# A hedgehog-attention and SwiGLU block: order of the wk transposes, evacuation of the folds, and the way of token tile 0

## The chip, the cores and the metric

One core of a Trainium2 chip runs the whole kernel. TensorE (PE in the profile) multiplies, ScalarE (ACT), VectorE (DVE) and GpSimd (POOL) do the elementwise work, and SyncE (SP) issues most of the DMAs. The metric is the device time in microseconds (us) of one execution; the median of several runs is compared.

## The reference

All values are bf16. Tokens S = 2048, width D = 640, 32 heads of 20, MLP width F = 1536.

```python
xn = layernorm(x)                        # no gain, no bias
q, k, v = split(xn @ wqkv)               # 32 heads of 20
pq, pk = q_h @ w_phi[h], k_h @ w_phi[h]  # per head, 20 x 20
phi = concat(softmax(p), softmax(-p))    # 40 features per head, for q and for k
kv, z = phi_k.T @ v, sum_s(phi_k)        # linear attention, not causal
attn = (phi_q @ kv) / (phi_q @ z + 1e-6) @ wo
mlp  = (silu(xn @ w1) * (xn @ w3)) @ w2
out  = x + attn + mlp
```

## The kernel before

Tokens lie in 16 tiles of 128. The kernel needs xn twice: by token (x_tok, normalised in place) and transposed (xnT, five chunks of 128 features by 2048 tokens), which all products with xn read. Tiles 4 to 15 are transposed by DMA (`turn`, line 693: one `dma_start_transpose` on SP). Tiles 0 to 3 are on the way to the first products, so they are handled apart: each is centred (`centre`), transposed on TensorE against an identity (`xc_transpose`) and used for the value rows (`v_pair`, `v_first`), and normalised (`ln_apply`) and transposed once more on TensorE for xnT (`xn_transpose`, line 857: five transposes into one PSUM bank, one evacuation). The tuple TURNED names those of the tiles 0 to 3 whose xnT comes by DMA instead (lines 1165 to 1171); it is empty.

The feature map w_phi is multiplied into wq and wk on the chip: `fold` (line 882) takes wq or wk transposed (wqkT, five chunks, each loaded by a transposing DMA from memory, `load_wT`, line 721) and a block-diagonal BDc that POOL builds from w_phi (phi_s), and writes Wkp (which = 1) or Wqp (which = 0). A fold uses two PSUM banks for the two halves of 320 columns, in six matmuls, and there are five folds for each of wk and wq. Key tiles (`k_tile`) are then xnT times Wkp, exponentiated on ACT; the MLP (`mlp`) works on blocks of 512 tokens and 128 of the 1536 hidden columns. Its weights w1_s and w3_s (w_s in the profile) come in four loads each of 384 columns, so the first pair allows three MLP units.

The order of the instructions is not written by hand. The function builds a list of operations with their data dependences and a level (priority) each; `_Program.schedule` (line 172) plays them on a table of prices: at each step every engine proposes the operation that could start first, and among those that could start within a small slack the one with the highest level. Where an operation has several ways (evacuations on ACT or DVE) the plan also chooses the engine. The slack is drawn at random from the seed SEED up to 175 us of planned time. The result is a fixed list for each engine, with semaphore waits. Queues are served in that order, so an instruction on SP that waits holds all DMAs behind it on SP.

The lines that set the start of the loads (`load_w13(0, 384)` issues w1's columns, then w3's):

```python
    n = len(P.all)
    load_w13(0, 384, lv - 4)
    for d in P.all[n:]:
        d.raw.add(chunk)
    first = [P.all[-1]]
    for e in range(DC):
        o = load_wT(1, e, lv - 9 - e, first)
        if e == 1:
            load(phi_s[:], phi_t, lv - 10.5, "SP", first)
    load_x(4, 8, lv - 19, "SP", [o])
```

The operations in `first` have to be complete before the wk transposes and phi are issued; the loads after them (x tiles 4 to 15, the other columns of w1 and w3, the wq transposes) wait for the last wk transpose. Levels: lv is 9e5; a transposing DMA of TURNED tiles has 2e6.

Of the kernel before, what the change touches and what calls it, by code (L numbers as in the profile page):

```python
# [4 lines left out]
ACT = mybir.ActivationFunctionType  # L5
# [5 lines left out]
D = 640  # L11
H = 32
DH = 20
F = 1536
T = S // 128
DC = D // 128
# [12 lines left out]
def heads_of_chunk(c):  # L29
    return (128 * c) // DH, (128 * c + 127) // DH  # L30
# [462 lines left out]
        return lists  # L493
CENTRED = {0: "ACT", 1: "ACT", 2: "ACT", 3: "DVE"}
POOLED = ()
TURNED = ()
SEED = 222
TRIPLES = ((0, 3, 0, 60), (3, 3, 60, 60), (6, 3, 120, 60), (9, 3, 180, 60), (12, 3, 240, 60), (13, 3, 300, 20))


def bass_parallel_sum__linear_kernel_hedgehog__glu_gated_swiglu__prompt_kernel(
# [13 lines left out]
    P = _Program(nc)  # L515
# [12 lines left out]
    def new(name, shape, dtype, offset=None):  # L528
        size = mybir.dt.size(dtype)
        for n in shape[1:]:  # L530
            size *= n
        return P.sbuf(name, shape, dtype, region(size) if offset is None else offset)
# [17 lines left out]
    xnT = new("xnT", [128, DC, S], bf)  # L550
    w1_s = new("w1_s", [128, DC, F], bf)
    w3_s = new("w3_s", [128, DC, F], bf)
    Wqp = new("Wqp", [128, DC, D], bf)
# [13 lines left out]
    Wkp = new("Wkp", [128, DC, D], bf, RKV)  # L567
    wv = new("wv", [128, DC, D], bf, RKV + 6400)
# [15 lines left out]
    v2 = new("v2", [128, T, H * 21 + 2], bf, RV)  # L584
# [14 lines left out]
    def bank(k, cols=512, off=0, p0=0, p1=128):  # L599
        return PS[p0:p1, k * 512 + off:k * 512 + off + cols]  # L600

    def bank2(k, cols):
        return PS[:, k * 512:(k + 2) * 512].rearrange("p (b c) -> p b c", c=512)[:, :, 0:cols]

    def free(ap):
        n = 1
        for s in ap.shape[1:]:
            n *= s
        return n
# [6 lines left out]
    def mm(j, o, l, r, start, stop, shared=False, busy=None):  # L616
        u, n = P.unit, free(r)

        def emit():
            return nc.tensor.matmul(o(u.k), l, r, start=start, stop=stop, skip_group_check=shared)  # L620
        return P.mm(emit, [l, r], j, max(n / 2400 + 0.0025, 0.035) if busy is None else busy, n)

    def way(eng, name, args, kw, busy, lat):
        u = P.unit
        e = {"ACT": nc.scalar, "DVE": nc.vector, "POOL": nc.gpsimd}[eng]

        def emit():
            return getattr(e, name)(*[at(a, u) for a in args], **{k: at(v, u) for k, v in kw.items()})  # L628
        emit.__name__ = name
        return eng, (emit, busy, lat)  # L630
# [5 lines left out]
    def sb(*aps):  # L636
        return [a for a in aps if hasattr(a, "ap")]

    def add(ways, w, r, banks=None, level=0.0, after=(), part=False):
        o = P.op(dict(ways), sb(*w), sb(*r), banks, level, after)  # L640
        o.part = part
        return o

    def w_act(o, i, f, n, scale=1.0, bias=None):
        kw = dict(scale=scale)
        if bias is not None:
            kw["bias"] = bias
        extra = 0.2 if hasattr(scale, "ap") or bias is not None else 0.0
        return way("ACT", "activation", (o, i, f), kw, 0.06 + n / 1200 + extra, 0.17 + n / 1200 + extra)

    def w_copy(o, i, n, fast=1):
        return way("DVE", "tensor_copy", (o, i), {}, 0.07 + n / 960 / fast, 0.15 + n / 960 / fast)
# [40 lines left out]
    def turn(o, i, level=0.0, dram=False, after=()):  # L693
        d = P.dma("SP", lambda: nc.sync.dma_start_transpose(o, i), sb(o), sb(i), *pieces(o, 256),  # L694
                  1.31, level, after)
        d.extra = 1.0 if dram else 0.2
        return d
# [23 lines left out]
    def load_wT(which, e, level, after=()):  # L721
        return turn(wqkT[:, which * DC + e:which * DC + e + 1, :],
                    A_wqkv[:, which * D + 128 * e:which * D + 128 * e + 128], level, True, after)
# [77 lines left out]
    def xc_transpose(t, level):  # L801
        n = 2 if t == 0 else 1
        u = P.begin(n, level)
        u.name = f"cT{t}"
        for dc in range(DC):
            l = xc[:, t, 128 * dc:128 * dc + 128]
            j, b = (0, dc) if n == 1 or dc < 3 else (1, dc - 3)

            def emit(l=l, j=j, b=b):
                a = (u.k + j) * 1024 + 128 * b  # L810
                return nc.tensor.transpose(PSb[:, a:a + 128], l, ident[:])
            P.mm(emit, [l, ident[:]], j, 0.056, 128)
        for j, a, b in ((0, 0, DC),) if n == 1 else ((0, 0, 3), (1, 3, DC)):
            def src(k, j=j, n=b - a):
                return PSb[:, (k + j) * 1024:(k + j) * 1024 + 128 * n].rearrange("p (c n) -> p c n", n=128)
            o = xcT[:, t, a:b, :]
            add([w_act(o, src, ACT.Copy, 128 * (b - a)), w_copy(o, src, 128 * (b - a), 2)], [o], [], [j], 1e6)
# [64 lines left out]
    def fold(which, dc, level):  # L882
        u = P.begin(2, level)
        u.name = f"fold{which}.{dc}"
        first = [True, True]
        for e in range(DC):
            h0, h1 = heads_of_chunk(e)
            lo, hi = DH * h0, DH * (h1 + 1)
            for q in range(2):
                a, b = max(lo, 320 * q), min(hi, 320 * q + 320)  # L890
                if a < b:
                    mm(q, lambda k, q=q, a=a, b=b: bank(k + q, b - a, a - 320 * q),
                       wqkT[:, which * DC + e, 128 * dc:128 * dc + 128],
                       BDc[:, e, a - lo:b - lo], first[q], e == DC - 1 or (q == 0 and e == 2), True)
                    first[q] = False

        if which:
            o = Wkp[:, dc, :].rearrange("p (b c) -> p b c", c=320)

            def src(k):  # L900
                return bank2(k, 320)
        else:
            o = Wqp[:, dc, :].rearrange("p (c r i) -> p r c i", r=2, i=64)

            def src(k):
                return bank2(k, 320).rearrange("p r (c i) -> p r c i", i=64)
        add([w_act(o, src, ACT.Copy, D), w_copy(o, src, D)], [Wkp[:, dc, :] if which else Wqp[:, dc, :]], [],
            [0, 1], 1e6)

    def v_half(t, q, level):  # L910
        u = P.begin(1, level)
        u.name = f"V{t}.{q}"
        for i in range(DC):
            mm(0, lambda k: bank(k, 320), xnT[:, i, t * 128:(t + 1) * 128], wv[:, i, 320 * q:320 * q + 320],
               i == 0, i == DC - 1)
        o = v2[:, t, 336 * q:336 * q + 336].rearrange("p (h c) -> p h c", c=21)[:, :, 0:DH]

        def src(k):
            return bank(k, 320).rearrange("p (h c) -> p h c", c=DH)
        add([w_act(o, src, ACT.Copy, 320), w_copy(o, src, 320)], [o], [], [0], 1e6)  # L920

    def proj(t, w):
        for i in range(DC):
# [209 lines left out]
    n = len(P.all)  # L1133
    load_w13(0, 384, lv - 4)
    for d in P.all[n:]:
        d.raw.add(chunk)
    first = [P.all[-1]]
    for e in range(DC):
        o = load_wT(1, e, lv - 9 - e, first)
        if e == 1:  # L1140
# [2 lines left out]
    n = len(P.all)  # L1143
# [14 lines left out]
    n = len(P.all)  # L1158
# [6 lines left out]
    for t in range(4):  # L1165
        if t in CENTRED:
            xc_transpose(t, 6e4 - 10 * t + 15)
        if t in TURNED:
            turn(xnT[:, :, t * 128:(t + 1) * 128], x_tok[:, t, :], 2e6)
# [18 lines left out]
    for dc in range(DC):  # L1188
        fold(1, dc, 4e4 - dc)
# [5 lines left out]
    n = len(P.all)  # L1195
# [3 lines left out]
    for dc in range(DC):  # L1199
        fold(0, dc, when(60 + 2 * dc))  # L1200
# [3 lines left out]
    for b in range(3):  # L1204
        for fc in range(FC):
            n = 12 * b + fc
# [6 lines left out]
    for b in range(NB):  # L1213
        for j in range(4):
            t = 4 * b + j
# [6 lines left out]

    P.schedule({"PE": 1.25, "ACT": 1.12, "DVE": 0.93, "POOL": 0.8, "SP": 0.81}, filler, 12.0, SEED, 175.0)

# [60 lines left out]
```

## Time and profile before

| | |
|---|---|
| median of 6 runs | 275.78 us (274.56 to 278.1) |
| profiled execution | 277.8 us, its span 276.1 us |
| mean TensorE clock of it | 0.994 of full |
| PE busy | 269.2 us, 97% of the span |
| DVE, ACT, POOL busy | 181.7, 105.0, 60.7 us |
| DMA | 21.98 MB, 31% of 16 engines for the hardware queue |

The profile names an instruction by engine, source line, operation and what it writes from what it reads; most instructions come from two helper lines, L620 (matmuls) and L628 (everything on ACT, DVE and POOL), so the names of the tiles tell them apart. L690 is a plain load or store, L694 a transposing DMA. SPq is SP issuing a DMA. "Idle before" is the time that the engine stood still ahead of an instruction, with what released it.

### The profile page before, as it was taken

Reading aid. Unit: us, or ns where it says so; the run is one execution under the profiler, and the core shown is the slowest. Engines: PE = TensorE matmul, PEld = TensorE weight load, DVE = VectorE, ACT = ScalarE, POOL = GpSimd, SP = SyncE. Lnnn points to the kernel's source line nnn. Section 1 sums busy time; section 2 is a strip of 40 time slices with the busy share of each in tenths; the row PEclk is TensorE's granted clock in tenths of the full one; section 3 lists DMA queues with packets and bytes.
Section 4 is the critical chain, followed back from the end, with each engine's and each line's share of the span. In section 5 each row is a group of like instructions: output and inputs, shape, how many; then the busy total and the mean of one; then the engine's idle time right before and its main releaser. Section 6 shows DMA issues by size and latency. Waiting matters only on the chain.

```text
span 276.1 us, 5052 instructions
## 1 busy us (share of the span) xinstructions
PE 269.2 (97%) x2077; PEld 160.5 (58%) x2095; DVE 181.7 (66%) x319; ACT 105.0 (38%) x191; POOL 60.7 (22%) x101
## 2 busy tenths in 40 slices
PE   8997999999999999999999999999999999999996
PEld 4746546677764446644444445767777775444774
DVE  5754799899997444478979797767761215566212
ACT  6633765577755441237573365010000001322000
POOL 4311273289999910000000000000000000000000
PEclk9997999999999999999999999999999999999999
DMA  7476999666000000711111111443332222000001
GB/s 223 134 99 197 338 252 150 137 80 210 2 0 2 0 0 2 241 48 26 38 36 24 24 26 25 77 116 98 96 91 77 74 71 74 0 0 0 26 24 48
DMA packets 41287, 21.98 MB, mean 80 GB/s; under 512 B 27056, under 2 KB 41264, under 8 KB 41264
## 3 DMA queue, kind: packets, MB, share of 16 engines
q1 hardware_dynamic: 40688, 21.01, 31.0%
q10 hardware_dynamic: 576, 0.66, 0.7%
q8 instruction: 16, 0.26, 0.4%
q14 instruction: 7, 0.06, 0.1%
HBM read 12.81 MB, written 2.62 MB: 56 GB/s over the span
## 4 chain that ended last, share of the span: by engine, by line
PE 88%; DMA 5%; SPq 3%; DVE 2%; issue 1%; ACT 0%
PE PS L620 88%; DMA w_s<-in_B_w_dram 3%; SPq L694 2%; DMA wv<-in_A_wqkv_dram 1%; DMA wqkT<-in_A_wqkv_dram 1%; DVE t L628 0%; SPq L690 0%; DVE hT L628 0%; DVE den_s L628 0%; ACT e_s L628 0%; DVE prod L628 0%; DVE g_s L628 0%; DVE xres L628 0%; DVE o_tok L628 0%; DVE pr_s L628 0%
## 5 line engine op out<-in xcount | busy, mean ns | idle before, releaser
L620 PE MATMUL PS<-xnT,w_s 128*128 128x512 bf16 x466 | 104.7, 379 | 1.2 <-issue 0.3
L620 PEld LDWEIGHTS PS<-xnT,w_s 128*128 128x128 bf16 x480 | 46.4, 98 | 55.0 <-DVE t L628 0.7
L628 ACT ACTIVATE th<-PS 128x512 f32<-128x512 f32 x48 | 28.7, 597 | 72.3 <-PE PS L620 72.1
L620 PE MATMUL PS<-w_s,hT 128*128 128x320 bf16 (+2 forms) x384 | 55.0, 299 | 0.0
L628 DVE SCALAR_TENSOR_TENSOR t<-th,PS 128x512 bf16<-128x512 f32 x48 | 32.8, 683 | 29.4 <-ACT th L628 29.2
L620 PEld LDWEIGHTS PS<-w_s,hT 128*128 128x128 bf16 x384 | 37.0, 98 | 14.8
L628 POOL TENSOR_TENSOR ekt<-ekt,rS 128x640 bf16<-128x640 bf16 x32 | 39.4, 1271 | 3.7 <-DVE rS L628 3.7
L628 DVE TENSOR_TENSOR xres<-PS,xres 128x640 bf16<-128x640 f32 (+2 forms) x17 | 13.3, 785 | 39.8 <-PE PS L620 39.8
L628 DVE SCALAR_TENSOR_TENSOR hT<-t,PS 128x512 bf16<-128x512 bf16 x48 | 32.8, 684 | 1.3
L628 ACT ACTIVATE EqT<-PS 128x512 bf16<-128x512 f32 x40 | 21.9, 595 | 12.4 <-PE PS L620 12.4
L620 PE MATMUL PS<-Wkp,xnT 128*128 128x320 bf16 x160 | 24.5, 304 | 0.0
L620 PE MATMUL PS<-wo_s,oT 128*128 128x320 bf16 (+2 forms) x160 | 24.5, 299 | 0.0
L628 ACT ACTIVATE ekt<-PS 128x640 bf16<-128x640 f32 x32 | 20.8, 701 | 9.3 <-PE PS L620 9.2
L628 DVE TENSOR_TENSOR prod<-PS,g_s 128x1280 bf16<-128x1280 f32 x16 | 23.8, 1490 | 0.6
L620 PE MATMUL PS<-xnT,Wqp 128*128 128x512 bf16 x96 | 23.1, 380 | 0.3 <-issue 0.2
L628 DVE TENSOR_REDUCE S<-ekt 128x64 f32<-128x1280 bf16 x16 | 22.8, 1444 | 0.5 <-ACT ekt L628 0.5
L628 ACT ACTIVATE e_s<-PS 128x64 f32<-128x64 f32 x32 | 9.0, 283 | 35.3 <-PE PS L620 34.8
L620 PEld LDWEIGHTS PS<-Wkp,xnT 128*128 128x128 bf16 x160 | 15.9, 100 | 6.3
L620 PEld LDWEIGHTS PS<-wo_s,oT 128*128 128x128 bf16 x160 | 15.7, 98 | 6.1
L620 PE MATMUL PS<-wv,xnT 128*128 128x320 bf16 x120 | 18.3, 299 | 0.0
L628 DVE BATCH_NORM_STATS2 bst<-x_tok 128x6 f32<-128x320 bf16 x32 | 14.1, 471 | 2.8 <-DMA x_tok<-in_A_x_dram 2.8
L620 PEld LDWEIGHTS PS<-xnT,Wqp 128*128 128x128 bf16 x100 | 9.3, 98 | 10.8
(68 smaller groups left out, 170.4 us busy)
## 6 DMA issues: line engine op xcount, KB each, us to landing
w_s<-in_B_w_dram SPq DMA_DIRECT2D x8, 480.0 KB, 6.9
xres<-in_A_x_dram SPq DMA_DIRECT2D x16, 160.0 KB, 2.2
out_dram<-xres SPq DMA_DIRECT2D x15, 160.0 KB, 1.8
x_tok<-in_A_x_dram SPq DMA_DIRECT2D x3, 640.0 KB, 7.6
w_s<-in_B_w_dram SPq DMA_DIRECT2D x1, 1920.0 KB, 9.1
wo_s<-in_A_wo_dram SPq DMA_DIRECT2D x1, 800.0 KB, 5.1
x_tok<-in_A_x_dram SPq DMA_DIRECT2D x2, 160.0 KB, 3.5
x_tok<-in_A_x_dram ACTq DMA_DIRECT2D x2, 160.0 KB, 3.8
```

The costliest lines, as they stand in the source:

```text
L620: return nc.tensor.matmul(o(u.k), l, r, start=start, stop=stop, skip_group_check=shared)
L628: return getattr(e, name)(*[at(a, u) for a in args], **{k: at(v, u) for k, v in kw.items()})
L694: d = P.dma("SP", lambda: nc.sync.dma_start_transpose(o, i), sb(o), sb(i), *pieces(o, 256), 1.31, level, after)
```

## The change

The wk transposes and phi wait for the first operation of the first w1 and w3 pair (w1's columns), not for the last (w3's). A fold leaves PSUM in two operations, one for each bank of 320 columns, each free to go to ACT or DVE, instead of one operation over both banks. Token tile 0 is listed in TURNED: its xnT columns come by a DMA transpose of x_tok on SP instead of five TensorE transposes and an evacuation. The seed of the planner is another. The unused function `v_half` is deleted.

```diff
-TURNED = ()
-SEED = 222
+TURNED = (0,)
+SEED = 385
...
-        if which:
-            o = Wkp[:, dc, :].rearrange("p (b c) -> p b c", c=320)
-
-            def src(k):
-                return bank2(k, 320)
-        else:
-            o = Wqp[:, dc, :].rearrange("p (c r i) -> p r c i", r=2, i=64)
-
-            def src(k):
-                return bank2(k, 320).rearrange("p r (c i) -> p r c i", i=64)
-        add([w_act(o, src, ACT.Copy, D), w_copy(o, src, D)], [Wkp[:, dc, :] if which else Wqp[:, dc, :]], [],
-            [0, 1], 1e6)
-
-    def v_half(t, q, level):
...
+        for q in range(2):
+            if which:
+                o = Wkp[:, dc, 320 * q:320 * q + 320]
+
+                def src(k, q=q):
+                    return bank(k + q, 320)
+            else:
+                o = Wqp[:, dc, :].rearrange("p (c r i) -> p r c i", r=2, i=64)[:, q, :, :]
+
+                def src(k, q=q):
+                    return bank(k + q, 320).rearrange("p (c i) -> p c i", i=64)
+            add([w_act(o, src, ACT.Copy, 320), w_copy(o, src, 320)], [o], [], [q], 1e6)
...
-    first = [P.all[-1]]
+    first = [P.all[n]]
```

More of the change, by code (lines that the diff above doesn't have):

```diff
@@ L895, in fold @@
                     first[q] = False
-        if which:
-            o = Wkp[:, dc, :].rearrange("p (b c) -> p b c", c=320)
-            def src(k):
-                return bank2(k, 320)
-        else:
-            o = Wqp[:, dc, :].rearrange("p (c r i) -> p r c i", r=2, i=64)
-            def src(k):
-                return bank2(k, 320).rearrange("p r (c i) -> p r c i", i=64)
-        add([w_act(o, src, ACT.Copy, D), w_copy(o, src, D)], [Wkp[:, dc, :] if which else Wqp[:, dc, :]], [],
-            [0, 1], 1e6)
-    def v_half(t, q, level):
[L911 to L920, printed above, removed]
+        for q in range(2):
[8 more added lines that the diff above has]
+            add([w_act(o, src, ACT.Copy, 320), w_copy(o, src, 320)], [o], [], [q], 1e6)
     def proj(t, w):
```

## The prediction

> **What bounds the kernel now.** I read the page first: busy shares, the 40 slices, the clock row.
>
> ```profile
> PE 269.2 (97%) x2077; PEld 160.5 (58%) x2095; DVE 181.7 (66%) x319; ACT 105.0 (38%) x191; POOL 60.7 (22%) x101
> ...
> PE   8997999999999999999999999999999999999996
> ...
> PEclk9997999999999999999999999999999999999999
> ```
>
> TensorE sets the time; the only dull slice is the fourth (20.7 to 27.6 us), both in busy share and in clock. Next, the chain of waits, for what releases TensorE there (start, us, what):
>
> ```profile
> 5.36 7.23 DMA w_s<-in_B_w_dram
> ...
> 12.61 1.24 SPq L694
> ...
> 13.89 2.37 SPq L694
> ...
> 16.30 0.58 SPq L690
> ...
> 19.49 3.08 DMA wqkT<-in_A_wqkv_dram
> 22.57 0.14 issue
> 22.70 8.56 PE PS L620 x65
> ```
>
> Up to 22.70 the chain is not arithmetic. It is the landing of w3's first columns at 12.59, five transposing loads of wk and the small load of phi issued one after another on SP, and the landing of the last transpose at 22.57. From there to the end it is nearly all TensorE. Third, TensorE's timeline there, and fourth the clock in short windows (second number: length; PEclk follows POOL):
>
> ```profile
> 20.15 0.57 PE L620 MATMUL PS<-BDc,wqkT 128*128 128x140 bf16 x2
> 20.90 0.25 PE L620 MATMUL PS<-BDc,wqkT 128*128 128x80 bf16 x2 [0.18 <-POOL BDc L628]
> 21.90 0.22 PE L620 MATMUL PS<-BDc,wqkT 128*128 128x140 bf16 x1 [0.75 <-DMA wqkT<-in_A_wqkv_dram]
> 22.70 2.49 PE L620 MATMUL PS<-BDc,wqkT 128*128 128x140 bf16 x25 [0.59 <-DMA wqkT<-in_A_wqkv_dram]
> 24.99 6.27 PE L620 MATMUL PS<-Wkp,xnT 128*128 128x320 bf16 x40
> 31.31 12.90 PE L620 MATMUL PS<-xnT,w_s 128*128 128x512 bf16 x58
> ```
>
> ```profile
> 22.50:23.00 0.50, 0.29 (x6) 0.33 (x7) 0.00 (x0) 0.04 (x1) 0.00 (x0) 0.94 0.00 0
> 23.00:26.00 3.00, 3.00 (x27) 2.58 (x25) 1.59 (x2) 1.97 (x3) 0.00 (x0) 0.50 0.67 204
> 26.00:26.50 0.50, 0.50 (x4) 0.28 (x3) 0.06 (x1) 0.00 (x0) 0.00 (x0) 0.65 1.07 366
> ```
>
> The three MLP units that the first columns of w1 and w3 allow end at 20.15. From there to 22.70 TensorE does five of the 30 fold matmuls and waits; then it runs at half clock to about 26.3. Its price: the 25 remaining folds take 2.29 us (22.70 to 24.99), where the wq folds later start six in 0.31 us (69.30 to 69.61), so 25 in 1.3: 1.0 lost. The four key tiles take 6.32 (24.99 to 31.31), where ten such matmuls start in 1.36 later (44.05 to 45.41), so 40 in 5.43: 0.9 lost. The hole thus costs 2.55 less 0.3 of folds, and 1.9 behind it.
>
> [...] the first x_tok transpose, issued at 31.11 behind loads, landed 7.3 us later at 38.4, 2.0 after the x load issued ahead of it (27.75 plus 8.7); with the queue empty such a transpose takes 2.7 to 3.1.
>
> **The change part by part.**
>
> *wk transposes behind w1.* The SP wait before them moves from the last of the pair to the first. This tile's answer gives w1's landing:
>
> ```profile
> L690 SPq DMA_DIRECT2D w_s<-in_B_w_dram x1: 379/379/379, 4.9 to 4.9; - x1
> ...
> DMA to landing us min/median/max: 6.3/6.3/6.3
> ```
>
> Issued at 4.94, landed at 11.24, against 12.59 for w3: the SP sequence (five transposes, phi) can start 1.35 earlier, the last wk chunk land at 22.57 - 1.35 = 21.2, phi at 18.3 and BDc on POOL be done at 20.3 instead of 21.6. All loads that wait for that last transpose (x tiles 4 to 7, the next w1 and w3 columns) move by the same 1.35. Bounds: no gain, if w3's remaining traffic slows the transposes by as much; up to 2.5, if the second transpose's long issue (2.37 against 1.24) falls away as well. I take 1.35.
>
> *Tile 0 by DMA.* Removed: five transposes of 0.44 us on TensorE at 9.35 and an ACT evacuation of 0.69 at 10.24. Both lie inside the V stage, whose end is set by tile 3's copies, so I count 0.1. Added: one transpose on SP, 1.24 of SP time, and a wait: the first MLP unit, and everything on TensorE's queue behind it, now needs its landing. x_tok tile 0 is normalised at 8.99 (DVE row 8.56, 0.43). If SP issues the transpose there, before the wk ones, SP is free again at 10.3, before w1's landing: it costs the wk sequence nothing. Its data lie behind w3's, so it lands between 12.6 + 1 and 12.6 + 2.0 = 14.6. I take 14.6; the MLP starts then instead of at 13.72, and its three units (13.72 to 20.15) end at 21.0, still ahead of 21.2. That cover gone, each us of landing after 14.8 costs one.
>
> *Folds by halves.* 10 evacuations of 640 columns (ACT 0.70, DVE 0.82) become 20 of 320. From ACT 0.595 at 512 and 0.70 at 640 columns, a half is about 0.44; from DVE 0.683 and 0.823, about 0.47. Per fold 0.91 engine us instead of 0.76, but two engines together free it after 0.47. For wk, five folds at 0.47 from 21.4 on leave the last chunk at 23.8, much as three whole ones of 0.70 on ACT would: nothing. It bounds the first key tile, whose fifth chunk must wait: it starts no earlier than 23.8 - 4 x 0.27 = 22.7. For wq (70 to 76 us) DVE gets up to 0.7 us more, while TensorE has other units in its order; the sums over heads that POOL waits for are due long before their use (POOL's last key product ends at 95.2, its reader starts at 107.5). Nothing, bounds 0 to 0.3.
>
> *SEED.* It redraws the planner's choices up to 175 us. After 24 us TensorE's own waits in the trace sum to 0.8 us (issue 0.5, DVE t 0.3), so a better draw gains under 1; a worse one may lose 1.5 by estimate. I take zero. v_half is called nowhere.
>
> *Sum.* Key tiles end at 22.7 + 0.1 + 5.43 = 28.2 instead of 31.3[...]: -3.1. If it still halves, -1.3. What is late next are w1's and w3's second columns: landed at 23.00 + 5.4 = 28.4 and 23.55 + 6.3 = 29.85 before, less 1.35 = 27.1 and 28.5; w3's half is used 1.1 after the unit begins, at 29.3. They just hold. So the profiled execution's 277.8 (span 276.1 and 1.7 around it) becomes 274.7. It is 2.0 above the median of 275.78, much the 1.9 that the low clock costs, so other executions may have escaped it: for those the gain is 31.3 - 1.9 - 28.2 = 1.2. Between 275.8 - 3.1 = 272.7 and 274.6, two to one for the low clock[...]: **273.3**, which is 0.9% down.
>
> **The rivals.**
>
> *Queue order (slower).* SP's order is written by the planner. With its own prices, used here for order only: w1 is due at about 9.0; DVE, in the order of this trace, ends tile 0's normalisation at about 9.2 (four pairs of statistics at 0.48 are put ahead of it). Unless a random slack of over 0.2 is drawn, or DVE's order changes, SP takes the first wk transpose first. On the chip that one waits for 11.24, so tile 0's is issued at 12.5 and lands 3.5 to 4.7 later (wqkT rows: 3.6, 4.6): 16.0 to 17.2. TensorE stands still from 13.6[...]: the units end at 17.2 + 6.4 + 1.7 = 25.3, folds and keys at 25.3 + 1.8 + 5.43 = 32.5, and the wk chunks land at 22.5 as now. Against 31.3 that is +1.2, against an execution without the low clock +3.1; at the early end, 0. Taken +1.9: **277.7**. It decides from a landing of tile 0 after about 15.5 on. For it: the planner's prices lie this close. Against: it takes 0.2 us to turn it round.
>
> *Hidden transfer.* The transposes start earlier but share 16 engines with w3's tail (DMA share 0.56 at 9 to 10, 0.25 and 0.09 after) and land no earlier, or the planner puts a fold ahead of the third MLP unit and the wait stands elsewhere. The edit then does not do what it says; **275.6**. Against: those shares are small.
>
> *A worse draw.* New waits of the query stage (the chain passes through e_s, den_s, g_s and prod at 156 to 163) eat the gain: 276.5.
>
> **How the numbers follow.** Forecast 0.56, queue order 0.24, hidden transfer 0.12, worse draw 0.08. The forecast's own range is 271.5 (the long issue gone too, the first unit at 13.6: 1 us more, and the low clock in all runs before) to 275.0. About 1% (2.8 us, limit 273.0) is what a measurement of this kernel can tell from no change, its runs spanning 274.56 to 278.1; six tenths of the forecast lie within it: faster 0.24, and 0.10 more for gains that the redraw adds. Slower by 1% (278.5): the upper part of the queue order 0.13 and of the worse draw 0.04. The range, 271.4 to 278.0, leaves out some 0.2.
>
> **What would show it.** Right: SP issues xnT before wqkT, wqkT's first issue at about 11.3, its last landing near 21.2, keys done near 28.2, clock 1.00 between 20 and 30, th after 14.6. Wrong: xnT tile 0 issued after 12 us, a hole on TensorE from 13.6 released by the xnT DMA, the half clock moved into the MLP units, or an MLP unit at 28 us waiting for w_s.

## The result, and the profile after

The changed kernel takes a median of 274.35 us (273.4 to 275.26, 36 runs) against 275.39 us (274.15 to 278.1, 73 runs) for the one before: ratio 0.9956, 95% interval 0.9943 to 0.9969. It is faster by 0.44%, 1.2 us by the ratio (1.04 between the medians). Its spread is 1.9 us, that of before 4.0. The six runs of before in the table further up had a median of 275.78; the 73 runs here put it at 275.39.

The profiled execution took 273.63 us (span 271.9), 4.2 less than the profiled one of before. The two profiles thus differ by 3.5 to 4 times as much as the kernels do. Most of what follows is about that factor. First the page of the profile after, busy shares, slices and clock:

```profile
PE 266.6 (98%) x2082; PEld 158.9 (58%) x2099; DVE 183.4 (67%) x326; ACT 104.3 (38%) x193; POOL 60.5 (22%) x101
...
PE   8999999999999999999999999999999999999996
...
PEclk9999999999999999999999999999999999999999
```

The dull fourth slice is gone, in busy share and in clock. TensorE's timeline of the same stretch, then the issues on SP (start, us, what):

```profile
13.44 6.42 PE L620 MATMUL PS<-xnT,w_s 128*128 128x512 bf16 x29
19.70 2.05 PE L620 MATMUL PS<-BDc,wqkT 128*128 128x140 bf16 x30
21.59 5.66 PE L620 MATMUL PS<-Wkp,xnT 128*128 128x320 bf16 x40
27.30 15.06 PE L620 MATMUL PS<-xnT,w_s 128*128 128x512 bf16 x68
```

```profile
5.18 0.95 SPq L690 DMA_DIRECT2D w_s<-in_B_w_dram  x2
6.36 1.31 SPq L694 DMA_TRANSPOSE xnT<-x_tok  x1
9.85 2.48 SPq L694 DMA_TRANSPOSE wqkT<-in_A_wqkv_dram  x2
12.37 1.58 SPq L690 DMA_DIRECT2D phi_s<-in_A_w_phi_dram  x1
13.99 3.84 SPq L694 DMA_TRANSPOSE wqkT<-in_A_wqkv_dram  x3
20.06 0.37 SPq L690 DMA_DIRECT2D x_tok<-in_A_x_dram  x1
```

The 30 folds follow the MLP units almost without a wait, at full clock, and the keys end at 21.59 + 5.66 = 27.25 instead of 24.99 + 6.27 = 31.26. The x load at 20.06 waits for wk's last chunk, so it shows that landing: 20.04, against 22.57 before. That is 2.5 us earlier, more than the 1.35 that the other wait is worth, because w1 itself landed 4.6 us after its issue in this execution and 6.3 in the one of before. The clock row of a short window (mean clock is the number after the five engines):

```profile
23.00:26.00 3.00, 3.00 (x24) 2.15 (x22) 1.74 (x6) 2.67 (x5) 0.00 (x0) 1.00 1.09 353
```

In the chain of waits of after the DMAs and SP have vanished from the opening; it is TensorE nearly throughout (start, us, what):

```profile
13.44 6.68 PE PS L620 x34
20.11 0.07 issue
20.18 7.07 PE PS L620 x65
```

The short break at 20.11 is what is left of the wait: the landing at 20.04 comes after the start of the first fold (19.70), not ahead of it.

One reading holds for all profiles below and makes them comparable. Let K be the end of the 40 key matmuls and E the start of the last addition, which is the last entry of the chain of waits, here in before and in after:

```profile
273.61 0.42 DVE xres L628
```

```profile
269.44 0.42 DVE xres L628
```

E - K depends on the plan, and hardly on the execution: 242.35 or 242.36 us in both profiles of before and in every kernel on its plan, 242.18 or 242.19 for the plan of after. The time of a profiled execution is E plus 4.2. If this holds for the executions without a profile too, a median of 275.39 stands for K = 28.8 and 274.35 for K = 28.0: the profiled executions, with 31.26 and 27.25, lay near opposite ends of what their kernels do.

### The profile page after: what moved, and what is told of

Its sections match the earlier page's. It is cut to its first block, busy times and chain, and to the rows that moved or that the text cites. A ratio compares the mean times of both kernels' runs of the same rounds, so it can differ in the third digit from the quotient of the medians.

```text
span 271.9 us, 5074 instructions
## 1 busy us (share of the span) xinstructions
PE 266.6 (98%) x2082; PEld 158.9 (58%) x2099; DVE 183.4 (67%) x326; ACT 104.3 (38%) x193; POOL 60.5 (22%) x101
## 3 DMA queue, kind: packets, MB, share of 16 engines
q1 hardware_dynamic: 41360, 21.17, 32.8%
## 4 chain that ended last, share of the span: by engine, by line
PE 94%; DVE 2%; ACT 2%; issue 1%
PE PS L620 92%; ACT EqT L628 2%; PE PS L1094 2%; PE PS L811 1%; DVE den_s L628 0%; DVE hT L628 0%; DVE t L628 0%; PE PS L865 0%; ACT e_s L628 0%; DVE o_tok L628 0%; DVE g_s L628 0%; DVE xres L628 0%; DVE pr_s L628 0%; DVE zero L628 0%; DVE prod L628 0%
## 5 line engine op out<-in xcount | busy, mean ns | idle before, releaser
L628 ACT ACTIVATE EqT<-PS 128x512 bf16<-128x512 f32 x40 | 21.8, 595 | 11.3 <-PE PS L620 11.3
L620 PE MATMUL PS<-Wkp,xnT 128*128 128x320 bf16 x160 | 23.9, 299 | 0.0
L628 ACT ACTIVATE ekt<-PS 128x640 bf16<-128x640 f32 x32 | 20.7, 698 | 7.5 <-PE PS L620 7.3
```

## The experiments

Where the text says "the plan with every instruction in its place", the planner ran as in the kernel named and one dependence was changed afterwards, ahead of writing out the lists; so nothing was redrawn. The wk transposes and phi are collected in `waiting`, w1's and w3's first loads are `w1_op` and `w3_op`.

### Is the first profile of before typical?

> The kernel before, unchanged, profiled a second time. Theory A (its profiled execution of 277.8 us was an unlucky one: w3's columns landed late, and the clock halved behind the hole): w3 lands nearer 11 us than 12.6, as in the profile after, the hole ahead of the folds is 0.5 to 1.5 us, the clock stays full, the key tiles end at 28 to 29 us instead of 31.3, and the total stays at a median of about 275.4. Theory B (the first profile was typical): w3 lands at 12.6, hole of 2.5 us, half clock, keys end at 31.3.

Measured: 275.84 us in the profiled execution, ratio to before 1.0012 (0.9989 to 1.0035). TensorE's timeline, and the start of the wk transposes on SP:

```profile
20.31 0.36 PE L620 MATMUL PS<-BDc,wqkT 128*128 128x140 bf16 x4
21.34 0.22 PE L620 MATMUL PS<-BDc,wqkT 128*128 128x140 bf16 x1 [0.67 <-DMA wqkT<-in_A_wqkv_dram]
22.05 1.51 PE L620 MATMUL PS<-BDc,wqkT 128*128 128x140 bf16 x25 [0.49 <-DMA wqkT<-in_A_wqkv_dram]
23.70 5.61 PE L620 MATMUL PS<-Wkp,xnT 128*128 128x320 bf16 x40
```

```profile
12.06 2.52 SPq L694 DMA_TRANSPOSE wqkT<-in_A_wqkv_dram  x2
```

Between the two theories: w3 landed at 12.05, late again, and the hole of about 1.5 us is there. But the clock stayed full: 25 folds start in 1.65 us and the keys take 5.61, so K = 29.31. Theory A's early landing did not show here, its full clock did. The two profiles also price the half clock: from the release of the 25 folds to K it is 8.56 us in the first (22.70 to 31.26) and 7.26 here (22.05 to 29.31), so 1.3 us, not the 1.9 of the prediction.

How often does it come? Of the 13 profiles of this study only the first one of before shows it. The mean clock of an execution says more: 3.4 us at half clock (mean 0.50 from 22.94 to 26.35) in 276 make it 0.994, the figure of the first profile. It is known for 156 more runs of before (14 here, 142 beside the experiments): one has 0.994 and takes 277.87 us, the others 0.999 or 1.0. So in these runs the half clock is a rare event and no part of the median. Of the 73 runs of the first comparison it is known for the profiled one alone; five of these took 277.46 us or more. What sets the half clock off is not shown: from the third MLP unit's end to the start of the half clock (20.15 to 22.94) TensorE was busy for 1.16 of 2.79 us by the trace, at full clock.

### The hole filled

```diff
+    first_fold = next(u for u in P.units if u.name == "fold1.0").mms[0]
...
     # hole: nine 128x512 matmuls on zeros into first_fold's bank;
     # they wait for that bank, not for wk
...
+    i = P.ops.index(first_fold)
+    P.ops[i:i] = hole
```

> The plan of before with nine more 512-column matmuls on zeros (1.9 us at full clock) between the third MLP unit and the first fold, so that TensorE does not fall idle there. Theory A: most executions have no half clock behind the hole, so the median hardly moves (275.2 to 275.8) and only the slow runs above 276.5 go. Theory D (the low clock behind the hole is in most executions): median 273.8 to 274.4, 1 us or more below before, PEclk 1.00 from 20 to 30 us.

Measured: median 276.12 us, ratio 1.0044 (1.0028 to 1.0060), spread 1.1 us.

```profile
20.31 2.10 PE L1229 MATMUL PS<-zero 128*128 128x512 bf16 x9
22.25 1.76 PE L620 MATMUL PS<-BDc,wqkT 128*128 128x140 bf16 x30
24.16 5.61 PE L620 MATMUL PS<-Wkp,xnT 128*128 128x320 bf16 x40
```

Theory D falls. Theory A's number misses too: it took the typical hole to be about as long as the filling, so that the median would hardly move. The run thus measures the typical hole. 1.94 us of work on zeros (20.31 to 22.25) cost 1.2 us by the ratio (1.45 between the medians, before being at 274.67 beside it). So in the median execution of before the hole, with whatever low clock stood behind it, was worth 0.5 to 0.7 us, not the 4 of the first profile. The filling also takes most of the spread upwards away: of its 22 runs none lies more than 0.5 us above their median, of the 59 runs of before beside it 19 do. Whether it takes the rare longest runs away as well (two of the 59 are above its highest, 276.61), 22 runs can't show.

### The wait on w3, by itself and in both directions

```diff
     # e_w1 and e_w1b: before's plan
+    for o in waiting:
+        o.raw.discard(w3_op)
+        o.raw.add(w1_op)
...
     # e_w3: after's plan
+    for o in waiting:
+        o.raw.discard(w1_op)
+        o.raw.add(w3_op)
```

> The plan of before with every instruction in its place; only the semaphore that SP waits on ahead of the wk transposes and phi is w1's. Theory A (the wait on w3 is the whole gain): wk's last chunk lands 1 to 1.4 us earlier, the hole closes, median 274.4, about 1.0 below before. Theory C (the gain comes from tile 0's DMA and the redrawn plan): 275.4, no change.

Measured: median 274.16 us against 274.67, ratio 0.9973 (0.9956 to 0.9990).

```profile
10.54 2.53 SPq L694 DMA_TRANSPOSE wqkT<-in_A_wqkv_dram  x2
...
19.64 0.37 SPq L690 DMA_DIRECT2D x_tok<-in_A_x_dram  x1
```

```profile
19.73 1.86 PE L620 MATMUL PS<-BDc,wqkT 128*128 128x140 bf16 x30
21.63 5.61 PE L620 MATMUL PS<-Wkp,xnT 128*128 128x320 bf16 x40
```

w1 landed at 10.5, wk's last chunk at 19.6, just ahead of the third MLP unit's end: no hole, K = 27.24, the same as in after's profile, with nothing but the semaphore changed. Theory C falls. The gain is 0.5 us between the medians and 0.7 by the ratio, not the 1.0 of theory A; it agrees with the worth of the hole by the filling.

> The plan of after with every instruction in its place; only the wait ahead of the wk transposes and phi is put back to w3. Theory A (the wait on w3 is the whole gain): the hole is back between the third MLP unit (ends near 19.9) and the folds, keys end 1 us later than 27.3 or more, median 275.3. Theory C (tile 0's DMA and the redrawn plan): 274.4.

Measured: 274.81 us, ratio to before 0.9993 (0.9971 to 1.0015): with the old wait after's plan is no longer measurably faster than before, and its median is 0.65 above that of e_w1 on the same chip. Its profiled execution had no hole, against my expectation: w3 landed at 11.2, and a slow start (below) had put the third unit's end to 20.7, where wk landed too.

> Before's plan with only the wait on w1, once more, beside after. Theory A (the wait is all of the gain but the 0.16 us that after's plan saves behind the keys): 0.1 to 0.2 us above after. Theory E (tile 0 by DMA or the halves bring several tenths more in the median): 0.4 us or more above after.

> After, unchanged, beside the two below on one chip. From the runs so far: total = end of the keys + what the plan does behind them (242.2 us for this plan to the last addition, 242.35 for that of before) + 4.2. About 0.4% below before, 274.0 to 274.5 if before is at 275.0 to 275.4.

On one chip, beside the same runs of before: e_w1b 274.36 us, ratio 0.9983 (0.9968 to 0.9998); after 273.99, ratio 0.9983 (0.9969 to 0.9997). The ratios are equal, and the medians lie 0.37 apart, between what theories A and E expected; so these runs neither show nor exclude a gain beyond the wait. After's own gain is smaller here than in the first comparison (0.17% against 0.44%, the intervals just meet; 0.60 us between the medians against 1.04): before ran at 274.59 instead of 275.39, after at 273.99 instead of 274.35.

### Tile 0, the halves, and the redrawn plans

```diff
     # e_turn: before with
-TURNED = ()
+TURNED = (0,)
...
     # e_whole: after with the fold of before (one operation of 640 columns)
...
     # e_seed130: after with
-SEED = 385
+SEED = 130
```

> Before with only token tile 0 by DMA (TURNED = (0,)); the wait on w3, whole folds and seed 222 stay, the plan is drawn anew. Theory A (the wait on w3 is the gain): the start of the first MLP unit and the hole behind the third stay as before, 275.0 to 275.6 against a median of about 275.2 for before. Theory C (tile 0 by DMA is worth several tenths, since five transposes and an evacuation leave the opening): the first MLP unit starts 0.3 us or more earlier, 274.6 or less.

> After with whole folds (one evacuation of 640 columns each, as before); the plan is drawn anew with seed 385. Theory A (halves are worth nothing): the keys start 1.7 us after the third MLP unit's end as in after, median 274.2 to 274.7. Rival (halves shorten the fold stage): keys start 0.3 us or more later, 274.7 to 275.2.

> After with another seed of the planner (130), whose planned span is 0.2 us shorter, with the first MLP unit planned 0.2 earlier. If the planner's ranking holds on the chip: 274.1, 0.2 below after, at the edge of what five rounds tell; if not, 274.3 to 274.7.

Measured: ratios to before 1.0029 (1.0015 to 1.0043), 1.0028 (1.0013 to 1.0042) and 1.0061 (1.0039 to 1.0084), all slower. The totals mislead; the table splits them at K (all from the profiled executions, K being start and length of the key group added). "Seen" is said of the first matmul because single records can be missing: e_turn, e_whole and e_seed130 show all 30 matmuls of the three units, the others 29, and the first one seen there is probably the second, 0.22 later:

| kernel | first MLP matmul seen | K | E | E - K |
|---|---|---|---|---|
| before | 13.72 | 31.26 | 273.61 | 242.35 |
| before_again | 14.05 | 29.31 | 271.66 | 242.35 |
| e_w1 | 13.47 | 27.24 | 269.60 | 242.36 |
| after | 13.44 | 27.25 | 269.44 | 242.19 |
| e_turn | 13.24 | 28.42 | 270.99 | 242.57 |
| e_whole | 14.02 | 28.01 | 271.63 | 243.62 |
| e_seed130 | 14.81 | 28.94 | 272.94 | 244.00 |

e_turn's first unit does not start 0.3 us earlier once the missing record is counted (13.24 here and 13.25 in e_w1, whose value stage starts at the same time, 5.96 and 5.95), so theory C falls there as well; 0.22 of what it loses lies behind K, the rest, in the opening, is not explained. e_whole's keys end at 28.01 after a late start, and it is 1.43 slower than after behind them, in a plan drawn anew: DVE hT appears in TensorE's waits from 40 to 270 us, which after's don't have at all. These waits are half of the 1.43.

```profile
PE PS L620 <- DVE hT L628: 0.7, 2, 0.4
```

In e_seed130 the same view shows one wait of 1.7 us:

```profile
PE PS L620 <- DVE t L628: 1.7, 1, 1.7
```

The seeds of before and after are both at the low end of this range, 0.16 apart; other draws cost up to 1.8. The planner's ranking did not hold: it put seed 130 0.2 us ahead. So the halves and tile 0 can't be read from these totals, only from the timeline of the opening:

*Halves.* Here are the folds and keys of after_again, then of e_whole:

```profile
20.50 1.82 PE L620 MATMUL PS<-BDc,wqkT 128*128 128x140 bf16 x30
22.16 5.67 PE L620 MATMUL PS<-Wkp,xnT 128*128 128x320 bf16 x40
```

```profile
20.49 1.86 PE L620 MATMUL PS<-BDc,wqkT 128*128 128x140 bf16 x30
22.40 5.61 PE L620 MATMUL PS<-Wkp,xnT 128*128 128x320 bf16 x40
```

Where wk has landed ahead of the first fold, the keys start 1.66 us after that fold with halves (after_again and e_queue; 1.67 in e_nowait) and 1.90 or 1.91 with whole folds (e_whole, e_w1, e_w1b, e_fill): halves are worth 0.24 us. In after's own profile the landing after the first fold hides this (19.70 to 21.59, 1.89). Where wk's last chunk releases 25 folds at once, the keys start 1.65 and 1.64 later with whole folds (before_again; e_turn, 21.17 to 22.81) and 1.32 with halves (e_seed130, 22.02 to 23.34): 0.3 us.

*Tile 0.* In before five transposes lie between two groups of the value stage; after has nine zero matmuls there, which the planner added as it saw a gap:

```profile
8.34 0.71 PE L620 MATMUL PS<-wv,xcT 128*128 128x320 bf16 x4
8.89 0.67 PE L1094 MATMUL PS<-zero 128*128 128x128 bf16 x9
9.39 1.52 PE L620 MATMUL PS<-wv,xcT 128*128 128x320 bf16 x10
```

From the four matmuls to the ten it is 1.05 us here, 0.86 in before (8.81 to 9.67). The freed time was filled, and 0.2 more. The plan of seed 130 has no zero matmuls there, and the 14 matmuls run on:

```profile
9.04 2.28 PE L620 MATMUL PS<-wv,xcT 128*128 128x320 bf16 x14
```

From the first of these to the last group of the value stage it is 3.23 us there (9.04 to 12.27), 3.33 in before (8.81 to 12.14), 3.35 in e_turn, which has six zero matmuls, and 3.52 in after (8.34 to 11.86). So leaving the five transposes out saves 0.1 us where nothing is put in their place, by one profile. After itself without its nine was not measured. In after they cost nearly what the halves save.

### The rival queue order

```diff
+    P.ops.remove(turned0)
+    P.ops.insert(P.ops.index(waiting[0]) + 1, turned0)    # after's plan
```

> The plan of after with one instruction moved: the DMA transpose of token tile 0 stands on SP behind the first wk transpose, so it is held by w1's landing. The rival queue order of the prediction: it is issued at 11 to 12.5 us and lands 3.5 to 4.7 later, the first MLP unit starts at 14.6 to 17 instead of 13.4, TensorE stands still ahead of it, wk's last chunk lands 1.3 later but no longer matters; 275.6 to 277.9, 1.3 to 3.5 above after. If a DMA transpose is absorbed by other work: 274.4.

Measured: 275.65 us, ratio to before 1.0040 (1.0016 to 1.0064). SP, then TensorE:

```profile
9.38 1.22 SPq L694 DMA_TRANSPOSE wqkT<-in_A_wqkv_dram  x1
10.65 1.26 SPq L694 DMA_TRANSPOSE xnT<-x_tok  x1
```

```profile
15.10 6.63 PE L620 MATMUL PS<-xnT,w_s 128*128 128x512 bf16 x30 [1.45 <-DMA xnT<-x_tok]
21.57 1.82 PE L620 MATMUL PS<-BDc,wqkT 128*128 128x140 bf16 x30
```

The mechanism is as forecast, in the lower half of its price (0 to 3.1): issued at 10.65, the tile's transpose lands at 15.0 and TensorE stands still 1.45 us. The clock stays full in this profile; of the nine runs one shows a mean clock of 0.994 and takes 277.7 us, 2 above the median, as in the first profile of before. One place in SP's queue turns a gain into a loss. And the planner does write this order: with seed 130 SP takes a wk transpose first as well.

```profile
14.81 6.63 PE L620 MATMUL PS<-xnT,w_s 128*128 128x512 bf16 x30 [1.01 <-DMA xnT<-x_tok]
```

### No wait at all

```diff
     # after's plan
+    for o in waiting:
+        o.raw.discard(w1_op)
```

The wait carries no data, it only holds the wk transposes back.

> After's plan with no wait at all ahead of the wk transposes and phi: SP issues them from about 7.7 us, while w1 and w3 are in flight. If descriptors queued behind w1 and w3 neither slow them nor are slowed: the first MLP unit starts as in after (13.2 to 14), wk's last chunk lands by 17, the folds never wait, and the executions in which w1 lands late lose their hole: median 0.2 to 0.4 us below after. If the transposes take engines from w3 or from token tile 0's transpose: the first MLP unit, or its w3 half, waits for a DMA, and the median is 0.3 us or more above after.

Measured: 273.68 us (273.33 to 274.42), ratio to before 0.9963 (0.9945 to 0.9981), on the chip where after had 0.9983.

```profile
6.52 1.30 SPq L694 DMA_TRANSPOSE xnT<-x_tok  x1
7.87 4.08 SPq L694 DMA_TRANSPOSE wqkT<-in_A_wqkv_dram  x2
...
19.12 0.37 SPq L690 DMA_DIRECT2D x_tok<-in_A_x_dram  x1
```

Issued 1.2 us earlier than in after_again (7.87 against 9.04), the wk transposes land no earlier (19.1 against 18.9, and not by 17 as expected): their first two issues held SP for 4.1 us, in after_again for 2.5. But w1, which here landed at 10.7 (issued at 4.74, 6.0 us), no longer sets their start. The median is 0.3 us below after's, but the two intervals overlap; the longest run is 274.42 of 12, in after_again 275.44 of 22, which is too few to tell. Its ratio is the lowest on this chip, but it is not shown to beat after.

## Why the prediction was right, and which term was off

The direction and the place came as forecast, 274.35 for 273.3 in a range of 271.4 to 278.0. That the range held says little, as it holds the time of before too; and the gain is less than half of the forecast one (1.04 between the medians, 2.5 forecast). So the mechanism was right and its size was not. By its steps:

*The wait on w3: right.* In the profiles where both landings can be read singly w3 landed 1.3 to 1.5 us after w1 (11.24 and 12.59 in before, 10.56 and 11.9 in e_w1, 9.8 and 11.3 in after); 1.35 was taken. Moving the semaphore alone gave a ratio of 0.9973 and 0.9983.

*Tile 0: order right, landing and worth off.* SP issued it ahead of wk, as the forecast assumed, but 2.6 us earlier than I placed it: DVE normalised tile 0 at 5.90, ahead of the other tiles' statistics, a draw of the plan and not a fixed order (in e_turn it was issued at 8.96). It landed at 6.36 + 5.6 = 12.0, 0.7 behind w3 (0.8 in after_again, 0.6 in e_nowait) and not 1 to 2.0, and bound nothing, where I had the first MLP unit wait until 14.6. The 0.1 gained on TensorE became 0.2 lost to zero matmuls.

*Halves: zero taken, 0.24 to 0.3 measured in the opening,* inside the bounds of 0 to 0.3. The two pieces were priced well (0.437 us on ACT and 0.480 on DVE for 0.44 and 0.47), but the forecast let the last evacuation end at much the same time either way. With whole folds the keys wait for it where the chain shows it (e_fill: ACT's last ends at 24.11, the keys start at 24.16); with halves the chain goes from folds to keys on TensorE alone (after_again, 14.24 to 27.83).

*Seed: zero taken, 0.16 gained.* My bound for a worse draw, 1.5, was a little small: 1.8 was measured.

*The step that was mis-sized is the last term of the sum*: how the profiled execution stands to the median. I set the low clock two to one into other executions, an estimate of mine that no trace or run here bears out. For the profiled pair the sum of 3.1, which takes the clock after the change for full (1.3 if it halves), was even too small: K fell by 4.0, of which 0.3 is the earlier start, 1.3 the clock and 2.4 the hole with the folds behind it. The clock was priced too high, at 1.9: in before_again, at full clock, the keys start 1.65 us after the release of the 25 folds and take 5.61, so the first profile lost 0.6 there and not 1.0 (2.29), and 0.7 in the keys and not 0.9 (6.27). The hole was priced too low, with 1.2 to be saved, as w1 landed early in after's profile. But the hole of before's profile was itself an extreme. The filled hole prices it at 0.5 to 0.7 in the median, and one run in 156 has the half clock. So the gain that I carried over as 2.1 to 2.5 is 1.04 between the medians of the first comparison, 0.9 in the opening and 0.16 behind, and 0.60 in the later one.

*Queue order.* I gave it 0.24 and a price of 1.9. It cost 1.1 by the ratio in e_queue; the half clock that I had put into it came in one run of nine.

*Hidden transfer.* It did not eat the gain: wk's last chunk landed 9.0 to 10.2 us after the first wk issue where that waited for w1 (e_w1, e_w1b, after, after_again), and 9.9 or 10.0 in the two profiles of before. Without any wait the earlier start was lost: 11.2 in e_nowait.

## What to carry to other kernels

When one profile is to be scaled to a median, look first where its own time lies in the spread of the runs: the 277.8 us of before lay at the top, so its waits were the worst ones and not the usual ones. A low clock seen in one profile should be looked for in the mean clock of the other runs before it is put into the median. A known amount of work on zeros put into a hole measures how wide the hole is in the median, which no single profile shows, provided that the work is longer than the hole. And where a planner redraws everything on each edit, change the dependence after planning, or cut the profile at a milestone, before believing a total: draws cost up to 1.8 us here, more than the change is worth.

## What the runs showed of the hardware that was not expected

A second source of the spread lies in the first 7 us, and no wait shows it. The chain of waits in after's profile, then in after_again, the same program:

```profile
5.04 0.38 PE PS L1094 x4
5.42 0.03 issue
5.45 0.45 PE PS L811 x5
5.90 2.33 PE PS L620 x16
```

```profile
5.42 0.75 PE PS L1094 x4
6.16 0.53 PE PS L811 x5
6.70 2.33 PE PS L620 x16
```

The same four zero matmuls take 0.38 or 0.75 us, and the value stage starts at 5.90 or 6.70, while the clock row reads 1.00 in both. The first MLP unit starts 0.8 us later (13.44, 14.24), and K is 0.6 later (27.25, 27.83), since the folds of after's profile lost 0.2 to wk's landing. Why the same matmuls take twice as long in one execution is not shown: the clock row does not have the slow stretch at all, and no run here moved it on purpose. The landing of w3's columns, 10.5 to 12.6 us in kernels that issue the same loads ahead of it, is another part of the spread; why it varies stays open.
